# A fused retention and hard-swish MLP kernel: Q 1 to 3 are sent later, together, and GpSimd casts two of them

## The chip, the cores and the metric

The kernel runs on one core of one Trainium2 chip. The metric is device microseconds of one execution, as a median over runs. The core has five engines that run on their own and wait for each other through semaphores: TensorE (PE, matrix products; PEld is its weight load), VectorE (DVE), ScalarE (ACT), GpSimd (POOL) and SyncE (SP). SP only issues DMAs here. GpSimd issues the DMAs that convert from float32 to float16 on the way.

## The reference

For 8 batches, 8 heads, 576 positions and a head dimension of 64, a retention layer without softmax, and then an MLP over all 4608 tokens (512 features, 2048 hidden):

```python
scores = scale * np.matmul(q, k.transpose(0, 1, 3, 2))      # scale = 1/8
gamma = 1.0 - 2.0 ** (-5.0 - np.arange(H))
Dmat = np.where(rel >= 0, gamma[:, None, None] ** rel, 0.0)  # rel = row - column
x = np.matmul(scores * Dmat, v)                              # tokens x 512
h = x @ w_in
out = (h * np.clip(h + 3.0, 0.0, 6.0) / 6.0) @ w_out
```

## The kernel before, in words

Each batch's first 512 positions are cut into four pieces of 128; the 64 positions left over in each batch are worked on in pairs of batches at the end. Piece c has tiles `kn` (K), and `qv` (Q in its first half, V in its second), all in float16 with positions on the partitions. The decay is split into a factor on Q and one on V, so that within a piece only a causal mask is left. What earlier pieces of the batch give is carried in a 64 x 64 state per head (`tbd`, as a block diagonal of two heads).

A piece goes through these steps:

- `k_by_pe(c)` transposes K on TensorE (tile `trk`), and ScalarE copies the result to `qk`.
- `q_by_pe(c)` multiplies Q with `dq`, an identity whose diagonal is the decay factor, which transposes and scales in one step (`trq`); ScalarE copies that to `qk` too. `dq` is made by VectorE near the start (L175).
- `scores(c)` makes K times Q (`sc`), and VectorE multiplies it with the mask (`at`).
- `scale_v(c)` scales V on VectorE. `state_early(c)` adds K times V to the state (`u`, through `gfull` to `tbd`).
- `inter(c)` and `intra(c)` give the output of the piece (`o`) from the state and from the masked scores, and ScalarE copies it to `xt`, the input of the MLP.

The four pieces of batch 0 (`EARLY = 4`) go first, written out by hand at L795 to L823; the last of them has its own versions `scores_last` and `out_last`, which mask and copy in two halves. Then the MLP of the first 512 tokens begins: `g1_first` and `g1` are the product with `w_in` (L577, 64 matmuls for a block of 512 tokens, four for each 128 hidden features), ScalarE and VectorE make the activation (L585, L586), and `g2` is the product with `w_out` (L635). From the third block on, `g2_seven` forms that product from seven instead of eight block products (L720). The pieces of later batches are placed between the matmuls of the MLP by hand.

The whole order is fixed by the program text (`manual_schedule`): each engine carries out its own instructions in the order in which they are written, and an instruction that waits holds up all that follow it on its engine. That holds for the DMA issues, too. GpSimd issues, in this order, K and V of pieces 0 to 3 (`load_kv`), then `w_in` in five blocks (`load_win`, 256, 256 and three times 512 hidden features), two blocks of `w_out`, piece 4, the rest of `w_out`, and the later pieces. Each of its issues also waits for the landing of the eighth issue before it. Q of pieces 0 to 3 (`load_q`) comes over SP in float32 into `qf`, and ScalarE casts it to `qv` (`cast_q`, L128). Before the change Q 0 and Q 1 are issued at once, Q 2 behind the transposes of Q 0, Q 3 behind those of K 0.

`warm(n, 512)` has TensorE multiply zeros, so that it does not stand idle.

At the end, the last block of tokens (`last`) keeps the accumulator `x` in two banks, `xo` and `xtu`, and `copy_half(u)` copies and stores each. The rows of this block belong to two batches, so `store_quarter` and `store` write each tile with two DMAs, one issued by SP and one by ScalarE.

Of the kernel before, what the change touches and what calls it, by code (L numbers as in the profile page):

```python
# [13 lines left out]
ALU = mybir.AluOpType  # L14
# [3 lines left out]
def kernel(  # L18
# [106 lines left out]
                reason="the first pieces have the queues")  # L125

    def cast_q(c):
        nc.scalar.copy(loaded[c]["q16"], plain_q[c])  # L128

    def load_win(f0, f1):  # L130
        return nc.gpsimd.dma_start(
# [11 lines left out]
    nc.gpsimd.iota(wide, pattern=[[1, P + 1]], base=-1, channel_multiplier=-1,  # L143
                   allow_small_or_imprecise_dtypes=True)
    load_q(0)
    load_q(1)
    load_kv(0)
    zeros = const.tile([P, MBLK], FP16)
    nc.vector.memset(zeros, 0.0)
# [6 lines left out]
    for h in range(H):  # L156
# [15 lines left out]
    nc.vector.tensor_tensor(out=ident16, in0=mask01, in1=mask_wide[:, 0:P], op=ALU.subtract)  # L172

    dq = const.tile([P, H, P], FP16)
    nc.vector.tensor_tensor(out=dq, in0=ident16[:, None, :].to_broadcast([P, H, P]),  # L175
                            in1=gq[:, :, None].to_broadcast([P, H, P]), op=ALU.mult)
    gqv = const.tile([P, 2, H, D], FP16)
    cast_q(0)
    nc.scalar.copy(gqv[:, 1], gv[:, :, None].to_broadcast([P, H, D]))
# [10 lines left out]
    nc.vector.memset(gfull, 0.0)  # L190

    def fill_gfull():
        nc.scalar.copy(gfull[0:HALF, :, 0:D],
                       gc[0:HALF, 0, :, None].to_broadcast([HALF, NPAIR, D]))
        nc.scalar.copy(gfull[HALF:P, :, D:2 * D],
                       gc[HALF:P, 0, :, None].to_broadcast([HALF, NPAIR, D]))

    def fill_gq():
        nc.scalar.copy(gqv[:, 0], gq[:, :, None].to_broadcast([P, H, D]))
# [52 lines left out]
    def k_by_pe(c, tag=None):  # L252
        kn = loaded[c]["kn"]
        pk = bank_or(tag, [P, NPAIR, P], FP16, name=f"trk_{c}")
        for p in range(NPAIR):
            newest[0] = nc.tensor.transpose(pk[:, p, :], kn[:, 2 * p:2 * p + 2, :], ident16)
        nc.scalar.copy(qk_of(c)[:, 1], pk)

    def q_by_pe(c):
        q16, qk = loaded[c]["q16"], qk_of(c)  # L260
        pq = bank([P, NPAIR, P], FP32, name=f"trq_{c}")
        for p in range(NPAIR):
            for h2 in range(2):
                r = slice(h2 * HALF, h2 * HALF + HALF)
                newest[0] = nc.tensor.matmul(
                    pq[r, p, :], q16[:, 2 * p + h2, :], dq[:, 2 * p + h2, :],
                    start=(p == 0), stop=(p == NPAIR - 1), skip_group_check=True)
        if c == EARLY - 1:
            for p in (0, 2):
                nc.scalar.copy(qk[:, 0, p:p + 2], pq[:, p:p + 2])  # L270
        else:
            nc.scalar.copy(qk[:, 0], pq)

    def scores_last(c):

# [60 lines left out]
    def scores(c, late=9):  # L336
        run_later(late)
        qk = st[c]["qk"]
        sc = psum.tile([P, 2, NPAIR, P], FP32, tag="sc", name=f"sc_{c}")
        for p in range(NPAIR):  # L340
            for h2 in range(2):
                r = slice(h2 * HALF, h2 * HALF + HALF)
                nc.tensor.matmul(sc[:, h2, p, :], qk[r, 1, p, :], qk[r, 0, p, :],
                                 start=True, stop=True)
        at = work.tile([P, 2, NPAIR, P], FP16, tag="at", bufs=3, name=f"at_{c}")
        st[c]["at"] = at
        later.append(lambda: nc.vector.tensor_tensor(
            out=at.rearrange("t a b s -> t (a b) s"), in0=sc.rearrange("t a b s -> t (a b) s"),
            in1=mask_b, op=ALU.mult))
# [328 lines left out]
    def store_quarter(kb, i, j, src):  # L678

        cols = slice(NH * j, NH * j + NH)  # L680
        if kb < B:
            r0 = kb * S + TH * i
            nc.sync.dma_start(out[r0:r0 + TH, cols].rearrange("(u p) n -> p u n", u=2), src)
        else:
            rest = out.rearrange("(m x s) n -> x s m n", x=2, s=S)
            for x in range(2):
                queue = nc.scalar if x else nc.sync
                queue.dma_start(rest[x, MAIN:S, 2 * i:2 * i + 2, cols],
                                src[x * HALF:x * HALF + HALF])

    def g2_seven(kb, last=False):

        gt = gts[kb]

        def w(i, j):
            return wout16[:, KH * i:KH * i + KH, NH * j:NH * j + NH]

        def a(i, j):
            return gt[:, KH * j:KH * j + KH, TH * i:TH * i + TH]

        def s(name):
            return sums[kb, name]

        acc = {}

        def get(name):
            if name not in acc:
                if last and name == "x":
                    acc[name] = [psum.tile([P, NH], FP32, tag=t, name=f"x{t}_{kb}")
                                 for t in ("o", "tu")]  # L710
                else:
                    whole = bank([P, 2, NH], FP32, name=f"{name}_{kb}")
                    acc[name] = [whole[:, 0], whole[:, 1]]
                    wholes[name] = whole
            return acc[name]

        def product(name, u, left, right, first):
            dst = get(name)[u]
            for c in range(KH):
                newest[0] = nc.tensor.matmul(  # L720
                    dst, left()[:, c, P * u:P * u + P], right[:, c, :],
                    start=(first and c == 0 and (u == 0 or name not in wholes)),
                    stop=(c == KH - 1), skip_group_check=True)

        kept, wholes = {}, {}

        def parts(name, tile):
            if name in wholes:
                return [(wholes[name], tile)]
            return [(acc[name][u], tile[:, u]) for u in range(2)]  # L730

        def keep(name):
            kept[name] = work.tile([P, 2, NH], FP32, tag="keep_" + {"m5": "m1"}.get(name, name), bufs=1,
                                   name=f"keep_{name}_{kb}")
            for src, dst in parts({"m5": "z"}.get(name, "x"), kept[name]):
                nc.scalar.copy(dst, src)

        def total(i, j, name, src):
            osb = work.tile([P, 2, NH], FP32, tag="osb", bufs=4, name=f"osb_{kb}_{i}_{j}")
            for (a0, dst), (_, a1) in zip(parts(src, osb), parts(src, kept[name])):  # L740
                nc.vector.tensor_tensor(out=dst, in0=a0, in1=a1, op=ALU.add)
            store_quarter(kb, i, j, osb)

        def copy_total():
            osb = work.tile([P, 2, NH], FP32, tag="osb", bufs=4, name=f"osb_{kb}_1_0")
            nc.scalar.copy(osb, wholes["x"])
            store_quarter(kb, 1, 0, osb)

        def copy_half(u):
            osb = work.tile([P, NH], FP32, tag="osb", bufs=4, name=f"osh_{kb}_{u}")  # L750
            nc.scalar.copy(osb, acc["x"][u])
            store(kb, 2 + u, slice(0, NH), osb)

        def unit(name, u, left, right, first, then=()):
            def do():
                product(name, u, left, right, first)
                for f in then:
                    f()
            return do

        plan = [
            ("x", lambda: a(0, 0), w(0, 0), True, [lambda: keep("m1")]),
            ("y", lambda: a(0, 1), w(1, 0), True,
             [lambda: total(0, 0, "m1", "y"), lambda: token_sums(kb, "s3")]),
            ("x", lambda: s("s2"), wts["t2"], False, [lambda: keep("u2")]),
            ("z", lambda: s("s1"), wts["t1"], True,
             [lambda: keep("m5"), lambda: token_sums(kb, "s4")]),
            ("x", lambda: s("s3"), wts["t3"], False, [lambda: total(1, 1, "m5", "x")]),
            ("z", lambda: s("s4"), w(1, 1), False, [lambda: total(0, 1, "u2", "z")]),
            ("x", lambda: a(1, 1), wts["t4"], False, [] if last else [copy_total]),  # L770
        ]
        units = []
        for n, (name, left, right, first, then) in enumerate(plan):
            for u in range(2):
                after = then if u else []
                if last and n == len(plan) - 1:
                    after = [lambda u=u: copy_half(u)]
                units.append(unit(name, u, left, right, first, after))
        return units
# [3 lines left out]
    WQ = DFF // 4  # L783
    for c in range(1, EARLY):
        load_kv(c)
    load_win(0, WQ // 2)
    load_win(WQ // 2, WQ)
    for i in range(1, 4):
# [3 lines left out]
            load(4)  # L792
        load_wout(4 * i, 4 * i + 4)

    scale_v(0)  # L795
    q_by_pe(0)
    load_q(2, newest[0])
    warm(2, MBLK)
    cast_q(1)
    k_by_pe(0)  # L800
    load_q(3, newest[0])
    fill_gfull()
    for c in range(EARLY):
        if c:
            inter(c - 1)
# [1 line left out]
        if c < EARLY - 1:  # L807
            scores(c)
            run_later(9)
            if c:  # L810
                k_by_pe(c + 1)
            state_early(c)
            run_later(9)
            if not c:
                k_by_pe(c + 1)
            q_by_pe(c + 1)
            if c + 2 < EARLY:
                cast_q(c + 2)
            scale_v(c + 1)
        else:  # L820
            scores_last(c)
# [280 lines left out]
```

## Time and profile before

| | us |
|---|---|
| median of 3 runs | 294.99 |
| the 3 runs | 293.27, 294.99, 295.82 |
| the profiled execution | 294.43 |
| its span | 292.6 |

The span runs from the first to the last instruction that the profiler shows; 1.8 us of the execution lie around it. All times within the kernel count from the start of the span. In it TensorE is busy for 281.1 us (96%), VectorE for 227.6, ScalarE for 169.1, GpSimd for 104.3, and the granted clock of TensorE is 1.00. Up to 18.16 us only the four first pieces are worked on; the MLP's first matmul starts at 18.17, and the last matmul ends near 287.7.

Queue 0 (software_dynamic) carries what GpSimd issues, queue 1 (hardware_dynamic) what SP issues. Packets of K, V and Q in queue 0 write 128 bytes, those of Q in queue 1 write 256. A share of 100% of 16 engines is one packet in work on each engine all the time; with several in work it is above that.

### The profile page before, as it was taken

What the parts mean: (1) busy time and instruction counts of PE and PEld (TensorE: products, weight loads), DVE (VectorE), ACT (ScalarE), POOL (GpSimd) and SP (SyncE); (2) the same over time, 40 slices, a digit from 0 to 9 for tenths busy, and PEclk for the clock granted to TensorE, in tenths of its full rate; (3) what the DMA queues carried; (4) which work ended last, traced back from release to release, by engine and by line L of the source; (5) the groups of instructions that cost most, each with busy time, mean ns of one, the idle gap of its engine ahead of it and who ended that gap; (6) DMA issues with size and microseconds to landing.
All of it is one profiled execution on the core that took longest, in us unless ns stands there. A gap on an engine that the chain in (4) does not pass through costs nothing.

```text
span 292.6 us, 8351 instructions
## 1 busy us (share of the span) xinstructions
PE 281.1 (96%) x3492; PEld 174.7 (60%) x3492; DVE 227.6 (78%) x377; ACT 169.1 (58%) x301; POOL 104.3 (36%) x130
## 2 busy tenths in 40 slices
PE   7699999999989999999999999999999999999993
PEld 2454445544544587458745874587458745874682
DVE  4858656798758997899789988998899588728860
ACT  6668537784357744774486448644864286338711
POOL 8753578159523432443234324455550000000000
PEclk9999999999999999999999999999999999999999
DMA  9999999999999989997999799979992240120014
GB/s 137 177 205 203 191 157 215 165 126 137 132 215 166 160 85 120 168 141 81 121 163 143 77 127 170 136 82 123 160 139 47 74 110 0 38 81 30 0 39 109
DMA packets 156631, 36.21 MB, mean 124 GB/s; under 512 B 143792, under 2 KB 155568, under 8 KB 156592
## 3 DMA queue, kind: packets, MB, share of 16 engines
q0 software_dynamic: 113104, 17.83, 89.3%
q1 hardware_dynamic: 42896, 17.31, 30.5%
q8 instruction: 27, 0.44, 0.7%
q10 hardware_dynamic: 592, 0.52, 0.5%
q14 instruction: 12, 0.10, 0.1%
HBM read 36.70 MB, written 9.44 MB: 158 GB/s over the span
## 4 chain that ended last, share of the span: by engine, by line
PE 91%; DMA 4%; POOL 2%; DVE 1%; issue 1%; ACT 0%; ACTq 0%; POOLq 0%
PE ph L577 41%; PE x L720 14%; PE pout L635 9%; PE z L720 8%; PE y L720 5%; DMA kn<-in_k_dram 3%; PE o L483 3%; PE sc L450 2%; PE o L504 1%; PE u L535 1%; PE ph L600 1%; POOL kn L103 1%; DMA out_dram<-osb 1%; PE xtu L720 1%; PE xo L720 1%
## 5 line engine op out<-in xcount | busy, mean ns | idle before, releaser
L577 PE MATMUL ph<-xt,win 128*128 128x512 f16 x560 | 122.3, 379 | 0.0
L586 DVE SCALAR_TENSOR_TENSOR gt<-u,ph 128x512 f16<-128x512 f32 x144 | 95.7, 685 | 22.6 <-ACT u L585 21.4
L585 ACT ACTIVATE u<-ph,cb 128x512 f32<-128x512 f32 x144 | 98.4, 688 | 25.7 <-PE ph L577 25.1
L577 PEld LDWEIGHTS <-win 128*128 128x128 f16 x560 | 54.7, 98 | 64.4
L103 POOL DMA_DIRECT2D kn<-in_k_dram x40 | 34.0, 850 | 40.7 <-PE ph L577 15.4
L103 POOL DMA_DIRECT2D qv<-in_v_dram x40 | 33.8, 846 | 38.8 <-PE ph L577 16.2
L720 PEld LDWEIGHTS <-sum_s 128*128 128x128 f16 x448 | 42.7, 98 | 5.3
L103 POOL DMA_DIRECT2D qv<-in_q_dram x36 | 30.2, 839 | 28.7 <-PE z L720 10.4
L720 PEld LDWEIGHTS <-gt 128*128 128x128 f16 x336 | 32.1, 98 | 5.5
L635 PE MATMUL pout<-wout,gt 128*128 128x512 f16 x128 | 29.6, 379 | 0.1
L720 PE MATMUL x<-wsum_t,sum_s 128*128 128x256 f16 x192 | 22.9, 273 | 0.0
L556 ACT CAST tm<-th 128x256 f16<-128x256 f32 x24 | 9.7, 405 | 20.3 <-DVE th L551 20.1
L635 PEld LDWEIGHTS <-gt 128*128 128x128 f16 x128 | 11.9, 98 | 13.2 <-issue 0.4
L456 DVE TENSOR_TENSOR at<-sc,mask 128x1024 f16<-128x1024 f32 x14 | 17.0, 1217 | 1.9 <-PE sc L450 1.9
L676 DVE TENSOR_TENSOR sum_s<-gt 128x1024 f16<-128x1024 f16 (+1 forms) x21 | 18.1, 864 | 0.2
L332 DVE TENSOR_TENSOR qv<-qv,gqv 128x1024 f16<-128x1024 f16 x26 | 17.8, 684 | 0.0
L514 ACT CAST xt<-o 128x512 f16<-128x512 f32 x28 | 15.0, 585 | 4.6 <-PE o L504 4.6
L567 DVE TENSOR_TENSOR ta<-u,th 128x256 f32<-128x256 f32 x24 | 10.2, 424 | 6.3 <-ACT th L554 5.2
L720 PE MATMUL z<-wout,sum_s 128*128 128x256 f16 x112 | 14.5, 274 | 0.0
L720 PE MATMUL y<-wout,gt 128*128 128x256 f16 x112 | 14.3, 273 | 0.0
L720 PE MATMUL z<-wsum_t,sum_s 128*128 128x256 f16 x112 | 13.6, 273 | 0.0
L720 PE MATMUL x<-wout,gt 128*128 128x256 f16 x96 | 11.5, 272 | 0.0
(118 smaller groups left out, 255.3 us busy)
## 6 DMA issues: line engine op xcount, KB each, us to landing
out_dram<-osb SPq DMA_DIRECT2D x32, 256.0 KB, 3.2
kn<-in_k_dram POOLq DMA_DIRECT2D x32, 128.0 KB, 5.9
qv<-in_v_dram POOLq DMA_DIRECT2D x32, 128.0 KB, 6.0
qv<-in_q_dram POOLq DMA_DIRECT2D x28, 128.0 KB, 5.9
wout<-in_moe_w_out_dram POOLq DMA_DIRECT2D x4, 512.0 KB, 15.2
win<-in_moe_w_in_dram POOLq DMA_DIRECT2D x3, 512.0 KB, 12.3
qf<-in_q_dram SPq DMA_DIRECT2D x4, 256.0 KB, 4.6
win<-in_moe_w_in_dram POOLq DMA_DIRECT2D x2, 256.0 KB, 8.3
```

Source lines behind the costliest of these rows:

```text
L103: loaded[c]["dma"].append(nc.gpsimd.dma_start(dst[p0:p0 + n], src[b, :, s0:s0 + n, :].rearrange("h s d -> s h d")))
L332: scaled = nc.vector.tensor_tensor(out=qv, in0=qv, in1=gqv, op=ALU.mult)
L456: nc.vector.tensor_tensor(out=at.rearrange("t a j p s -> t (a j p) s"), in0=sc.rearrange("t a j p s -> t (a j p) s"), in1=mask64[:, None, ...
L514: nc.scalar.copy(xt_at(cs[0], 0, 2 * P).rearrange("e p (j x s) -> e p j x s", j=2, x=2) [:, :, :, half, :], o[half].rearrange("e j p s -> ...
L556: nc.scalar.copy(tm, ta)
L567: nc.vector.tensor_tensor(out=ta, in0=st[c]["u"][1], in1=st[c]["sum"], op=ALU.add)
L577: newest[0] = nc.tensor.matmul(ph, win16[:, dmc, P * fc:P * fc + P], xt_of(kb)[:, dmc, :], start=(dmc == 0), stop=(dmc == NCC - 1))
L585: nc.scalar.activation(u, ph, ACTF.Relu, bias=cb[:, 0:1], scale=1.0 / 6.0)
L586: nc.vector.scalar_tensor_tensor(out=gts[kb][:, fc, :], in0=u, scalar=1.0, in1=ph, op0=ALU.min, op1=ALU.mult)
L635: nc.tensor.matmul(pout, gt[:, fc, P * mc:P * mc + P], wout16[:, fc, :], start=(fc == 0), stop=(fc == NFC - 1))
L676: nc.vector.tensor_tensor(out=s(which)[:, c0:c1], in0=x(), in1=y(), op=op)
L720: newest[0] = nc.tensor.matmul(dst, left()[:, c, P * u:P * u + P], right[:, c, :], start=(first and c == 0 and (u == 0 or name not in whol ...
```

## The change

- Q 1 is issued behind the making of the diagonal `dq`, and Q 2 and Q 3 right behind Q 1, without a wait of their own.
- The casts of Q 2 and Q 3 go from ScalarE to GpSimd, where they stand between the issue of V 3 and the first of `w_in`.
- The cast of Q 1 goes behind the copy of K 0 on ScalarE; the two fills of `gfull` go from ScalarE to VectorE; one more warming matmul stands behind the transposes of K 0.
- In piece 0, V is scaled behind the mask of the scores, and the state is updated behind the transposes of piece 1. In piece 2, the state comes first, and Q 3 is transposed before K 3; the copy that is cut into halves is that of K 3 instead of Q 3.
- In the last block of tokens, the second half of quarter (0,1) is stored by GpSimd instead of ScalarE, and the last copy, of `xtu`, is made by VectorE instead of ScalarE.
- `newest`, to which later loads are tied, is no longer set by `q_by_pe`, and is set by `scores`. The loads that use it come behind matmuls of L577 or L720, so that it holds the same instruction there.

```diff
     def cast_q(c):
-        nc.scalar.copy(loaded[c]["q16"], plain_q[c])
+        (nc.scalar.copy if c < 2 else nc.gpsimd.tensor_copy)(loaded[c]["q16"], plain_q[c])
...
     load_q(0)
-    load_q(1)
     load_kv(0)
...
-    nc.vector.tensor_tensor(out=dq, in0=ident16[:, None, :].to_broadcast([P, H, P]),
-                            in1=gq[:, :, None].to_broadcast([P, H, P]), op=ALU.mult)
+    load_q(1, nc.vector.tensor_tensor(
+        out=dq, in0=ident16[:, None, :].to_broadcast([P, H, P]),
+        in1=gq[:, :, None].to_broadcast([P, H, P]), op=ALU.mult))
+    for c in range(2, EARLY):
+        load_q(c)
...
     def fill_gfull():
-        nc.scalar.copy(gfull[0:HALF, :, 0:D],
+        nc.vector.tensor_copy(gfull[0:HALF, :, 0:D],
...
     (k_by_pe)
-        nc.scalar.copy(qk_of(c)[:, 1], pk)
+        if c == EARLY - 1:
+            for p in (0, 2):
+                nc.scalar.copy(qk_of(c)[:, 1, p:p + 2], pk[:, p:p + 2])
+        else:
+            nc.scalar.copy(qk_of(c)[:, 1], pk)
...
     (q_by_pe)
-        if c == EARLY - 1:
-            for p in (0, 2):
-                nc.scalar.copy(qk[:, 0, p:p + 2], pq[:, p:p + 2])
-        else:
-            nc.scalar.copy(qk[:, 0], pq)
+        nc.scalar.copy(qk[:, 0], pq)
...
     (store_quarter)
-                queue = nc.scalar if x else nc.sync
+                queue = (nc.gpsimd if j > i else nc.scalar) if x else nc.sync
...
         def copy_half(u):
-            nc.scalar.copy(osb, acc["x"][u])
+            if u:
+                nc.vector.tensor_copy(osb, acc["x"][u])
+            else:
+                nc.scalar.copy(osb, acc["x"][u])
...
     for c in range(1, EARLY):
         load_kv(c)
+    for c in range(2, EARLY):
+        cast_q(c)
     load_win(0, WQ // 2)
...
-    scale_v(0)
+    fill_gfull()
     q_by_pe(0)
-    load_q(2, newest[0])
     warm(2, MBLK)
-    cast_q(1)
     k_by_pe(0)
-    load_q(3, newest[0])
-    fill_gfull()
+    warm(1, MBLK)
     for c in range(EARLY):
...
             run_later(9)
-            if c:
-                k_by_pe(c + 1)
-            state_early(c)
-            run_later(9)
             if not c:
-                k_by_pe(c + 1)
-            q_by_pe(c + 1)
-            if c + 2 < EARLY:
-                cast_q(c + 2)
+                cast_q(1)
+            else:
+                state_early(c)
+                run_later(9)
+            if not c:
+                scale_v(c)
+            if c == EARLY - 2:
+                q_by_pe(c + 1)
+            k_by_pe(c + 1)
+            if c < EARLY - 2:
+                q_by_pe(c + 1)
+            if not c:
+                state_early(c)
+                run_later(9)
             scale_v(c + 1)
```

More of the change, by code (lines that the diff above doesn't have):

```diff
@@ L192, in fill_gfull @@
     def fill_gfull():
-        nc.scalar.copy(gfull[0:HALF, :, 0:D],
-                       gc[0:HALF, 0, :, None].to_broadcast([HALF, NPAIR, D]))
-        nc.scalar.copy(gfull[HALF:P, :, D:2 * D],
-                       gc[HALF:P, 0, :, None].to_broadcast([HALF, NPAIR, D]))
+        nc.vector.tensor_copy(gfull[0:HALF, :, 0:D],
+                              gc[0:HALF, 0, :, None].to_broadcast([HALF, NPAIR, D]))
+        nc.vector.tensor_copy(gfull[HALF:P, :, D:2 * D],
+                              gc[HALF:P, 0, :, None].to_broadcast([HALF, NPAIR, D]))
     def fill_gq():
@@ L264, in q_by_pe @@
                 r = slice(h2 * HALF, h2 * HALF + HALF)
-                newest[0] = nc.tensor.matmul(
-                    pq[r, p, :], q16[:, 2 * p + h2, :], dq[:, 2 * p + h2, :],
-                    start=(p == 0), stop=(p == NPAIR - 1), skip_group_check=True)
-        if c == EARLY - 1:
-            for p in (0, 2):
-                nc.scalar.copy(qk[:, 0, p:p + 2], pq[:, p:p + 2])
-        else:
-            nc.scalar.copy(qk[:, 0], pq)
+                nc.tensor.matmul(pq[r, p, :], q16[:, 2 * p + h2, :], dq[:, 2 * p + h2, :],
+                                 start=(p == 0), stop=(p == NPAIR - 1), skip_group_check=True)
+        nc.scalar.copy(qk[:, 0], pq)
     def scores_last(c):
@@ L342, in scores @@
                 r = slice(h2 * HALF, h2 * HALF + HALF)
-                nc.tensor.matmul(sc[:, h2, p, :], qk[r, 1, p, :], qk[r, 0, p, :],
-                                 start=True, stop=True)
+                newest[0] = nc.tensor.matmul(sc[:, h2, p, :], qk[r, 1, p, :], qk[r, 0, p, :],
+                                             start=True, stop=True)
         at = work.tile([P, 2, NPAIR, P], FP16, tag="at", bufs=3, name=f"at_{c}")
```

## The prediction

> **What bounds the kernel now.** I read the page first, then the chain of waits for the first 20 us, then the DMA queues over short windows, then the timeline of the last ten microseconds.
>
> ```profile
> span 292.6 us, 8351 instructions
> ...
> PE 91%; DMA 4%; POOL 2%; DVE 1%; issue 1%; ACT 0%; ACTq 0%; POOLq 0%
> ```
>
> TensorE (PE) is the chain. From 18.2 us on it runs almost without a gap to 287.7; the diff leaves that part alone, so its 269 us are a block that can only be shifted. What the diff touches is the start, up to the first matmul of the MLP (L577), and the end, after the last one. The start's chain, in order of time (start, length, what):
>
> ```profile
> 6.75 7.55 DMA kn<-in_k_dram
> ...
> 14.34 0.40 PE trk L256 x4
> ...
> 15.18 0.34 PE trq L265 x8
> ...
> 16.20 0.37 PE sc L283 x8
> ...
> 16.59 1.30 DVE at L286 x2
> ...
> 18.23 1.83 PE ph L577 x8
> ```
>
> K 3 is the last load to matter: it is issued at 6.75 and lands at 14.30, and 3.8 us of transposes, scores and masks follow it. Why it takes 7.55 us is in the queues. First window 6 to 7 us, then 7.5 to 9 (queue, packets, MB, share):
>
> ```profile
> q0 software_dynamic: 1175, 0.15, 232.6%
> ...
> qf<-in_q_dram SPq DMA_DIRECT2D x1, 256.0 KB, 6.8
> ```
>
> ```profile
> q1 hardware_dynamic: 888, 0.23, 96.3%
> q0 software_dynamic: 428, 0.05, 55.9%
> ```
>
> Queue 0 (GpSimd's loads) alone moves 1175 packets per us. With a Q of queue 1 beside it the sum falls to 1316 in 1.5 us, 877 per us (948 in the window 10.5 to 12). A load of K, V or Q is 1024 packets, so the engines are full from 1.9 to 13.65 us with eight K and V and four Q. The same bytes move after the change; only their order can help.
>
> The end (timeline: start, length, engine):
>
> ```profile
> 284.71 2.64 ACTq L688 DMA_DIRECT2D out_dram<-osb  x2
> ...
> 285.80 1.04 PE L720 MATMUL xo<-wsum_t,gt 128*128 128x256 f16 x8
> ...
> 286.67 1.04 PE L720 MATMUL xtu<-wsum_t,gt 128*128 128x256 f16 x8
> 287.45 0.37 ACT L751 COPY osh<-xo 128x256 f32<-128x256 f32 x1 [4.30 <-DMA out_dram<-osb]
> ...
> 288.49 0.37 ACT L751 COPY osh<-xtu 128x256 f32<-128x256 f32 x1 [0.66 <-ACT osh L751]
> 288.89 0.51 ACTq L625 DMA_DIRECT2D out_dram<-osh  x1
> ```
>
> The sums are ready at 286.84 and 287.71, yet ScalarE copies them at 287.45 and 288.49. Each copy starts 0.10 to 0.12 after ScalarE's own issue of a store ends (284.71 + 2.64 = 287.35; 287.86 + 0.51 = 288.37). The DMA named as releaser is a neighbour in time.
>
> **The end, part by part.** The second half of the store of quarter (0,1) moves from ScalarE to GpSimd, and the last copy moves to VectorE. ScalarE is then free when `xo` is done: copy at 286.9 instead of 287.45. VectorE, idle after 286.69, takes `xtu` at 287.74 (its L741 began 0.03 after `xtu` at 284.22). For that copy the trace has ScalarE's 0.37 and L741's 0.42 with two inputs; I take 0.42: store issued at 288.21 instead of 288.89. That is 0.68, and I count **0.65 gained**. GpSimd's store must not become last. It is issued at 286.72; a GpSimd load of 64 KB issued near 201 us landed after 3.0, so it lands at 289.7, against 290.4 for the last one (issue 288.21 plus 2.2, the median landing of such stores). If it needed over 3.7 us, as in the full queues of the start, the gain would be gone.
>
> **The start: the loads.** Q 1 is now issued after `dq`, which ends at 3.60 (2.37 + 1.23), and Q 2 and 3 follow at once on SP, 0.37 to 0.56 each: issues at 3.65, 4.2 and 4.7. Nothing else stands behind them on SP until the store near 42 us.
> - Queue 1 is empty from 2.97 (1024 packets at 1080 per us from 1.9), so queue 0, which began at 4.0, begins then. K 0 lands near 5.2 instead of 6.12. It is worth nothing: TensorE has its two warming matmuls until 6.2 in front of the transposes. They were hidden before by K 0 and are now the limit; the extra warming matmul lies under ScalarE's 0.59 copy.
> - In the trace the first packets of Q 2 come 2.0 us after its issue (5.33, then 7.3), those of Q 3 3.6. I take 2.0: 5.65. By then queue 0 has moved 2.68 x 1150 = 3080 packets (K 0, V 0, K 1).
> - From 7.3 to 12.3 the old kernel moved some 4930 packets, 986 per us, 42% of them queue 1's. With three Q waiting I take half: 3120 / 493 = 6.3 us, so queue 1 ends at 12.0. Landing is 1.1 to 1.5 us behind the last packet. Q 1 lands at 8.5, Q 2 at 10.6, Q 3 at 13.1. Bounds: 10.9 + 1.1 = 12.0 at the 592 per us of the window above, and 14.3 if each Q takes the 2.85 us that lay between the starts of Q 2 and Q 3.
> - K 2 then lands at 11.1 (it was 11.04), V 2 at 13.3 (12.85), K 3 at 14.4 (14.30), V 3 at 15.15 (15.1).
>
> **The start: GpSimd's casts.** They are in no row. From below stands VectorE's 0.42 for 512 elements, from above GpSimd's iota (129 elements in 0.24) scaled to 0.95; I take 0.66, the iota's slope over its 0.10 memset. Cast 2 ends at 11.3, and TensorE wants it at 12.0. Cast 3 ends at 13.8, wanted at 14.5. Behind them on GpSimd wait all of w_in, then w_out and pieces 4 to 7:
>
> ```profile
> 8.48 3.79 POOL L131 DMA_DIRECT2D win<-in_moe_w_in_dram  x5
> ...
> 20.71 0.75 POOL L136 DMA_DIRECT2D wout<-in_moe_w_out_dram  x1 [1.48 <-DMA win<-in_moe_w_in_dram]
> ```
>
> w_in's first issue goes from 8.48 to 13.85, its first packet (0.84 after the issue, as near 63 us, where the queue was empty) from 13.65 to 14.7: 1.05 later, with the engines idle for 0.85. Its third block landed at 20.5 (issue 9.96 + 10.5) and is wanted 3.46 after the first MLP matmul (16 matmuls of 0.216): at 21.6, slack 1.1 to 1.2. The second has 1.8, the fourth 2.1; later, Q 5 lands 1.3 before its use at 41.39. So the move costs **nothing in my sum**, with no cover left: each later microsecond costs one.
>
> **The start: the order of the work.** Cast 1 now stands behind the copy of K 0 on ScalarE and ends at 9.1; Q 1's transposes, the state update and the output of piece 0 (0.41 each) come after it, scores 1 at 10.4 instead of 9.52. That is hidden, since the next thing waits for K 2 at 11.1. The two fills of `gfull` leave ScalarE (0.80) for VectorE, which is idle from 5.2 to 7.1. Piece 2: transposes, two copies of 0.59, scores at 13.0; but VectorE scales V 2 first (13.3 + 0.42) and masks until 15.0 (it was 14.6). Piece 3: Q is transposed before K (0.41 off the tail of K 3), K at 14.9; ScalarE copies Q 14.95 to 15.55, then half of K, 15.9; TensorE's output of piece 2 waits for that mask, until 16.0; VectorE has the state (0.69) and V 3 (0.42) until 16.2. Scores until 16.4, mask at 16.5 instead of 16.59: **0.1 gained**. What the new order saves behind K 3 is given back in front of it.
>
> **Sum.** 0.65 + 0.1 + 0 = 0.75 less. The profiled execution took 294.43 (span 292.6 and 1.8 around it), which gives 293.7. The median of the three runs is 0.56 higher, 294.99, so on that footing **294.2**. Those runs spread over 2.55 us; about 1% (2.95) is what can be told from no change.
>
> **Rivals.**
> 1. *w_in too late* (slower). The Q take turns with queue 0 as in the old trace, Q 3 lands at 14.3 and its cast, at 0.95, ends at 15.25. w_in starts at 16.15, 2.5 late; its third block lands at 23.0, and the MLP, 3.46 in, stops for it: 1.3 behind the old time at that place. Less 0.65: 0.65 slower, **295.6**. It decides from a cast end of 13.95 on. For it: Q 3 needed 6.8 us with less queued. Against it: the three are now queued together, as Q 0 and Q 1 were, which ran from 1.9 to 4.1 with 56 packets of queue 0 between.
> 2. *Even sharing.* Q 1's packets come 1.2 us after issue, as the first Q's did, and split the engines from 4.85: queue 0 has 2160 packets then, K 2 ends at 10.9 and lands at 12.2; scores 2 at 13.9, masks until 15.55, the last mask at 16.95, 0.35 late. Less 0.65: **294.7**. Against it: in the window 6 to 7 queue 1 had none, though Q 2 was issued at 5.33. The Trainium skill (DMA: Bandwidth & Descriptors, Queues, rings and completion order) says that an engine takes the queues in turn, a packet of at most 64 descriptors each; by that rule this rival would hold, and this window does not agree with it.
> 3. *Less mixing* (faster). If the Q run in one piece, the 12,300 packets need 7.2 + 3.9 us and end at 13.0, K 3 lands at 13.6, Q 3 near 11, and the chain behind is 0.9 earlier: with the end 1.6 less, **293.4**. Against it: both mixed windows.
> 4. *No end gain.* GpSimd's store lands last, or the chain at the start takes what the end gives: **295.0**.
>
> **Chances.** My sum 0.37, rival 1 0.25, rival 2 0.13, rival 3 0.11, rival 4 0.14. With the spread of the runs, half of 2.55, around the outer cases and rival 1 growing with a slower cast: 292.9 to 296.4. Over 1% faster (below 292.0) needs more than rival 3: 0.04. Over 1% slower (above 297.9) needs w_in some 5 us late: 0.09. Within 1%: 0.87.
>
> **What would show it.** Right: Q 3's cast ends between 13 and 14, w_in is issued at once after it, the last masks start near 16.5 and L577 near 18.1 without a gap; the last store is issued near 288.2 if nothing shifts. Wrong: a gap in L577 between 19 and 26 that w_in ends (rival 1), K 2 after 12 (2), K 3 before 14 (3), a last landing that is GpSimd's (4). GpSimd casts above 1.5 us each would break the sum.

## The result, and the profile after

The changed kernel takes 296.61 us (median of 8 runs, 296.0 to 298.14) beside 293.94 for the kernel before (median of 8, 293.05 to 295.82): 1.0091 times as long, with a 95% interval of 1.0067 to 1.0115. The forecast of 294.2 and its range up to 296.4 were too low, and where a gain was forecast there is a loss. The profiled execution took 296.60.

First the span, the granted clock in 40 slices, and the shares of the chain by engine, from the page of after:

```profile
span 294.8 us, 8356 instructions
...
PEclk9599999999999999999999999999999999999999
...
PE 82%; DMA 12%; POOL 1%; DVE 1%; issue 1%; SPq 0%; ACT 0%; DVEq 0%
```

The span is 2.2 longer. DMA has 12% of the chain, where it had 4%, and the second slice (7.4 to 14.7 us) has a clock of 0.5. The chain of waits at the start of after (start, length, what) runs elsewhere than before:

```profile
4.67 10.02 DMA qf<-in_q_dram
14.69 0.05 issue
14.74 0.61 POOL qv L128
15.35 3.62 POOL win L131 x5
18.98 13.10 DMA wout<-in_moe_w_out_dram
...
32.38 12.49 DMA qv<-in_q_dram
```

It no longer goes through K 3. It is Q 3, issued at 4.67 and landed at 14.69, then its cast on GpSimd, then the issues of `w_in` behind that cast. From there it runs on through GpSimd's queue: the first load of `w_out` lands at 32.08, only then is Q 5 issued (32.38, before 28.29), the load lands at 44.87, and TensorE's transposes of Q 5 start behind it, at 44.91. What waits for these loads shows in the timeline of after from 15 to 46 us (start, length, engine; in brackets the idle time before and what ended it):

```profile
15.30 3.73 POOL L131 DMA_DIRECT2D win<-in_moe_w_in_dram  x5
...
19.78 3.63 PE L578 MATMUL ph<-xt,win 128*128 128x512 f16 x16
...
24.48 0.55 PEld L578 LDWEIGHTS <-win 128*128 128x128 f16 x4 [1.57 <-DMA win<-in_moe_w_in_dram]
24.49 0.82 PE L578 MATMUL ph<-xt,win 128*128 128x512 f16 x3 [1.08 <-DVE gt L587]
...
44.91 0.41 PE L271 MATMUL trq<-dq,qv 128*64 128x128 f16 x8 [0.58 <-DMA qv<-in_q_dram]
```

The MLP starts at 19.78 instead of 18.17. Its weight loads then wait for the third block of `w_in`, which landed at 24.44 (the stop that the matmul row puts down to `gt` is the same one). Later Q 5, which stands behind `w_in` and `w_out` in GpSimd's queue, stops TensorE for another 0.58.

Where the time went, each row as a difference of the same instruction in the two traces:

| what | before | after | added |
|---|---|---|---|
| first matmul of the MLP | 18.17 | 19.78 | +1.61 |
| the 17th matmul of the MLP, the first that needs the third block of `w_in` | 21.63 | 24.49 | +1.25 |
| first product with `w_in` of the second block of tokens (Q 5 in between) | 52.08 | 55.61 | +0.67 |
| last matmul's end (a wait near 85 us was 0.94, is 0.25) | 287.71 | 290.33 | -0.91 |
| from there to the end of the span | 4.94 | 4.47 | -0.47 |

The sum is +2.15. The first three rows give each delay to the place where it shows; they are not three savings that could be had one by one. The chain reaches the transposes of Q 5, at 44.91 instead of 41.39, without any matmul of the MLP in it. So an earlier start of the MLP alone would only have made the later stops longer; in one run below it starts 1.15 later than here, and Q 5 is reached at the same time.

Why the MLP starts late stands in the windows of after (window, length, busy time and count of PE, PEld, DVE, ACT, POOL, then granted clock, DMA share, GB/s):

```profile
6.83:9.58 2.75, 0.01 (x2) 0.00 (x1) 1.56 (x2) 0.62 (x1) 1.71 (x2) 0.76 1.84 196
9.58:15.30 5.72, 5.71 (x61) 3.80 (x61) 3.22 (x5) 2.90 (x5) 1.17 (x2) 0.52 1.81 145
```

and in its timeline:

```profile
8.89 0.62 ACT L128 CAST qv<-qf 128x512 f16<-128x512 f32 x1 [2.51 <-DMA qf<-in_q_dram]
9.58 0.61 PE L258 MATMUL trk<-ident,kn 128*128 128x128 f16 x4 [2.75 <-DMA kn<-in_k_dram]
...
14.74 0.61 POOL L128 CAST qv<-qf 128x512 f16<-128x512 f32 x1 [2.79 <-DMA qf<-in_q_dram]
...
16.57 0.40 PE L258 MATMUL trk<-ident,kn 128*128 128x128 f16 x4
...
18.20 1.29 DVE L287 TENSOR_TENSOR at<-sc,mask_wide 128x512 f16<-128x512 f32 x2 [0.29 <-PE sc L284]
```

TensorE stands idle for 2.75 us waiting for K 1 (landed 9.54, before 7.91). Then it is busy without a gap for 5.7 us, at a clock of 0.52: the four transposes take 0.61 where they take 0.40 at 16.57. So a backlog forms. K 3 lands at 15.73 (before 14.30), and its transposes start 0.84 behind that instead of 0.04. The queues say why the loads are late: from 5 to 14 us (queue, packets, MB, share)

```profile
q0 software_dynamic: 6009, 0.76, 131.2%
q1 hardware_dynamic: 3110, 0.78, 51.7%
```

are 1013 packets per us, of which the three Q have a third. The share was not even: from 5.5 to 9 us queue 1 moved 1792 of 3458 packets, from 9 to 13 us 1190 of 4119, and its last ones came after 14. And the engines that were full all the time before have nothing to do when GpSimd at last issues `w_in`; from 15.5 to 16.5 us:

```profile
DMA packets 64, 0.01 MB, mean 8 GB/s; under 512 B 64, under 2 KB 64, under 8 KB 64
```

At the end, the timeline of after:

```profile
289.29 1.04 PE L721 MATMUL xtu<-wsum_t,gt 128*128 128x256 f16 x8
289.49 0.37 ACT L755 COPY osh<-xo 128x256 f32<-128x256 f32 x1 [3.73 <-PE xo L721]
289.62 0.62 POOL L689 DMA_DIRECT2D out_dram<-osb  x1 [69.10 <-DVE osb L742]
...
290.37 0.43 DVE L753 COPY osh<-xtu 128x256 f32<-128x256 f32 x1 [1.06 <-PE xtu L721]
```

ScalarE copies `xo` as soon as it is done, VectorE copies `xtu` 0.04 after the last matmul, and the last store is issued 0.49 after it (1.18 before).

### The profile page after: what moved, and what is told of

Same layout as the page of the kernel before. It is cut to its first block, busy times and chain, and to the rows that moved or that the text cites. A ratio compares the mean times of both kernels' runs of the same rounds, so it can differ in the third digit from the quotient of the medians.

```text
span 294.8 us, 8356 instructions
## 1 busy us (share of the span) xinstructions
PE 283.1 (96%) x3493; PEld 175.8 (60%) x3493; DVE 228.8 (78%) x380; ACT 167.0 (57%) x296; POOL 105.9 (36%) x133
## 4 chain that ended last, share of the span: by engine, by line
PE 82%; DMA 12%; POOL 1%; DVE 1%; issue 1%; SPq 0%; ACT 0%; DVEq 0%
PE ph L578 36%; PE x L721 14%; PE z L721 9%; PE pout L636 6%; PE y L721 5%; DMA wout<-in_moe_w_out_dram 4%; DMA qv<-in_q_dram 4%; DMA qf<-in_q_dram 3%; PE o L484 2%; PE sc L451 2%; PE o L505 1%; PE u L536 1%; PE ph L601 1%; POOL win L131 1%; PE xtu L721 1%; PE xo L721 1%
## 5 line engine op out<-in xcount | busy, mean ns | idle before, releaser
L689 POOL DMA_DIRECT2D out_dram<-osb x1 | 0.6, 617 | 69.1 <-DVE osb L742 69.1
L677 DVE TENSOR_TENSOR sum_s<-gt 128x1024 f16<-128x1024 f16 (+1 forms) x21 | 18.1, 863 | 0.2
L721 PE MATMUL z<-wout,sum_s 128*128 128x256 f16 x112 | 14.5, 274 | 0.0
L721 PE MATMUL y<-wout,gt 128*128 128x256 f16 x112 | 14.3, 274 | 0.0
```

The source lines that it names most:

```text
L677: nc.vector.tensor_tensor(out=s(which)[:, c0:c1], in0=x(), in1=y(), op=op)
L721: newest[0] = nc.tensor.matmul(dst, left()[:, c, P * u:P * u + P], right[:, c, :], start=(first and c == 0 and (u == 0 or name not in whol ...
```

## The experiments

Four theories, which may hold together. **H, the hold:** `w_in` stands behind a cast that waits for Q 3, so it is issued 6.8 us later. **S, the sends:** three Q queued together delay K 1, K 2 and Q 3, and the MLP starts late. **K, the clock:** most of what S costs comes from the halved clock, not from the landings. **C:** the cast is itself dear on GpSimd. The kernels of one group shared one chip and the runs of the kernel before (medians 294.63, 294.56 and 294.88); ratios are against that kernel.

### First group: each part by itself

**The end alone**, in the kernel before:

```diff
-                queue = nc.scalar if x else nc.sync
+                queue = (nc.gpsimd if j > i else nc.scalar) if x else nc.sync
...
-            nc.scalar.copy(osb, acc["x"][u])
+            if u:
+                nc.vector.tensor_copy(osb, acc["x"][u])
+            else:
+                nc.scalar.copy(osb, acc["x"][u])
```

> The kernel before with the two edits of its end alone: the second half of the store of quarter (0,1) by GpSimd, the copy of xtu by VectorE. If the end of the changed kernel gains what its trace shows (from the last matmul to the end of the span 4.47 us, before 4.94), this kernel is 0.45 to 0.65 us faster than before, a ratio of 0.998, with the last store issued 0.5 us behind the last matmul instead of 1.18. If the end costs (GpSimd's store lands last), it is at 1.000 or above. The first MLP matmul stays at 18.2 in both cases.

Measured: 0.9982 (0.9957 to 1.0008), 294.19 us. The last store is issued 0.50 after the last matmul, as in after. A gain of half a microsecond fits, but is not told from none.

**The changed kernel with the casts back on ScalarE:**

```diff
-        (nc.scalar.copy if c < 2 else nc.gpsimd.tensor_copy)(loaded[c]["q16"], plain_q[c])
+        nc.scalar.copy(loaded[c]["q16"], plain_q[c])
...
-    for c in range(2, EARLY):
-        cast_q(c)
...
+            if c + 2 < EARLY:
+                cast_q(c + 2)
```

> The changed kernel with the casts of Q 2 and Q 3 back on ScalarE, behind the transposes of Q 1 and of Q 2; the Q are still sent together. Theory H (w_in is held behind the casts): w_in is issued from 8.5 again, its third block lands before 22, TensorE does not stop in the first MLP product, and piece 5 is not late at 45; 1.8 us of the loss go, and the rest, some 0.9, stays, because the first MLP matmul is still near 19.5. Theory S (sending the three Q together is the whole loss, by making K, V and Q late): the first MLP matmul stays at 19.5 to 20 and so does nearly the whole loss, a ratio of 1.007 or more. Theory O (the new order of the work is slower by itself): the same as S here.

Measured: 1.0053 (1.0026 to 1.0079), 296.18 us. `w_in` is issued from 8.47 and no product waits for it, nor for Q 5, yet the MLP starts at 20.18. TensorE is idle from 7.11 to 9.88 and then has a clock of 0.5. That is S without H.

**The changed kernel with the sends as before:**

```diff
+    load_q(1)
...
-    load_q(1, nc.vector.tensor_tensor(
...
-    for c in range(2, EARLY):
-        load_q(c)
...
     q_by_pe(0)
+    load_q(2, newest[0])
...
     k_by_pe(0)
+    load_q(3, newest[0])
```

> The changed kernel with the Q sent as before (Q 1 at once, Q 2 behind the transposes of Q 0, Q 3 behind those of K 0), and the casts still on GpSimd ahead of w_in. Theory H: Q 3 lands near 13.4 as before, its cast ends near 14.1, w_in starts 1.2 us late instead of 3; the third block lands near 21.7 and TensorE stops for 0.2 to 0.5 us; together with the end, -0.5 to +0.2 us against before. Theory S: the whole loss goes, the first MLP matmul is at 18.2 or earlier, a ratio of 0.996 to 0.999. Theory O: the loss stays, the first MLP matmul above 19.

Measured: 1.0076 (1.0050 to 1.0103), 296.72 us. Here the MLP starts on time and then stops for `w_in`. GpSimd's and TensorE's timelines of this kernel:

```profile
13.46 0.61 POOL L128 CAST qv<-qf 128x512 f16<-128x512 f32 x1 [2.11 <-DMA qf<-in_q_dram]
14.02 3.73 POOL L131 DMA_DIRECT2D win<-in_moe_w_in_dram  x5
```

```profile
18.17 1.90 PE L577 MATMUL ph<-xt,win 128*128 128x512 f16 x8
20.97 1.90 PE L577 MATMUL ph<-xt,win 128*128 128x512 f16 x8 [0.90 <-DMA win<-in_moe_w_in_dram]
23.51 0.82 PE L577 MATMUL ph<-xt,win 128*128 128x512 f16 x3 [0.65 <-DMA win<-in_moe_w_in_dram]
```

That is H without S. It is also nearly what the prediction took for its own case (`w_in` from 13.85, at no cost); the second block, said to have 1.8 of slack, came 0.9 late. Q 5 then stops TensorE for another 0.84, until 44.31. The clock was halved in this profile, too, from 9.9 to 13.3, but the MLP starts at 18.17 as before, and the three other runs, with a mean granted clock of 1.00, took 295.91 to 297.66. So the clock is not what this kernel loses by.

**Both back**, so that the new order of the work and the end remain (the edits of the last two):

> The changed kernel with both the sending and the casts as before: what is left is the new order of the work and the end. Theories H and S: the loss is gone; the first MLP matmul lies between 17.6 and 18.2, no stop in the first product; 0.5 to 1.1 us faster than before, a ratio of 0.996 to 0.998. Theory O: slower than before by 0.5 or more, the first MLP matmul after 18.7. H beside S: H expects this one 0.2 to 0.5 us below the kernel with the sends alone put back; S expects no difference.

Measured: 0.9979 (0.9960 to 0.9998), 293.57 us, MLP from 17.84. So neither the new order nor the end costs anything. Against this kernel, S alone adds 0.74% and H alone 0.97%, and the changed kernel with both is 1.1% above it (its ratio is from another chip). They overlap, because one path ends last: where `w_in` is held, the landing of Q 5 sets the place at 44 us (44.31 with the sends as before, 44.91 in after), and a late start of the MLP lies under it.

### Second group: what makes the hold and the sends dear

**Both casts behind all five issues of `w_in`**, otherwise as changed:

```diff
-    for c in range(2, EARLY):
-        cast_q(c)
     load_win(0, WQ // 2)
...
         load_win(i * WQ, i * WQ + WQ)
+    for c in range(2, EARLY):
+        cast_q(c)
```

> The changed kernel with the five issues of w_in ahead of the two casts on GpSimd instead of behind them; the Q are sent together as in the changed kernel. Theory H (the hold of w_in is a cost of its own): no stop of TensorE in the first MLP product, which still begins at 19.5 to 20.2; the time is that of the kernel with the casts back on ScalarE, a ratio near 1.005, below the changed kernel's 1.009. Theory C (it is the cast on GpSimd itself that costs, by its length or by getting in the way of VectorE, wherever it stands): no better than the changed kernel, 1.008 or more.

Measured: 1.011 (1.0057 to 1.0162), 298.38 us. GpSimd's timeline shows that the test missed its aim:

```profile
11.84 0.74 POOL L131 DMA_DIRECT2D win<-in_moe_w_in_dram  x1 [1.07 <-DMA qv<-in_v_dram]
13.64 0.74 POOL L131 DMA_DIRECT2D win<-in_moe_w_in_dram  x1 [1.06 <-DMA kn<-in_k_dram]
14.38 1.38 POOL L128 CAST qv<-qf 128x512 f16<-128x512 f32 x2
```

The fourth and fifth issue of `w_in` wait for earlier landings, and now the casts wait behind them. Q 2, landed at 10.68, is cast at 14.38; TensorE loses 1.04 to that, and the MLP starts at 21.79. The hold is turned round.

**TensorE kept busy** in the kernel with the casts back:

```diff
             if not c:
+                warm(11, MBLK)
                 cast_q(1)
```

> The kernel with the Q sent together and the casts on ScalarE, with eleven more warming matmuls (of zeros) behind the scores of piece 0, which fill 2.4 us of the 2.77 us in which TensorE stood idle. Theory K (the halved clock from 8.8 to 15.7 that followed this idle time makes a good part of the 2.0 us by which the MLP begins late): the granted clock stays at 1.0, the transposes of Q 3 begin 0.3 to 0.8 us earlier, the first MLP matmul comes before 19.6, and the ratio falls from 1.0053 to 1.003 or 1.004. Theory L (the late landing of Q 3 and K 3 alone sets the start): the clock stays up and the first MLP matmul is still within 0.2 us of 20.2, the ratio near 1.005.

Measured: 1.0014 (0.9983 to 1.0045), 295.19 us. Two windows of the kernel with the casts back, then the same two of this one:

```profile
7.11:9.88 2.77, 0.00 (x1) 0.01 (x1) 1.56 (x2) 0.62 (x1) 2.77 (x4) 0.81 1.75 186
9.88:15.70 5.82, 5.81 (x61) 3.88 (x61) 3.27 (x5) 3.75 (x7) 2.79 (x5) 0.50 1.98 162
```

```profile
7.11:9.88 2.77, 2.44 (x15) 1.01 (x14) 1.23 (x2) 0.62 (x1) 2.77 (x4) 1.00 1.81 186
9.88:15.70 5.82, 4.78 (x80) 3.12 (x78) 4.10 (x6) 4.16 (x8) 3.39 (x6) 1.00 1.98 167
```

DMA share and GB/s hardly change, but with zeros to multiply the clock stays at 1.00, and the second window holds 80 matmuls instead of 61. The MLP starts at 18.92 instead of 20.18. Of the 2.34 us that the sends cost at that place (17.84 with both back), 1.26 went with the clock. Not all of that need be the clock's, since K 3 landed about 0.7 earlier in the second profile (15.1 beside 15.8); in the first its transposes start 1.14 behind its landing. The other runs agree: the mean granted clock was 0.994 to 1.000 in the ten runs of this kernel and 0.985 to 0.994 in the eight with the casts back. K holds there for about half of what the sends cost, not for most of it, and the intervals of the two ratios (1.0014 and 1.0053) still overlap.

**The sends as before, the casts between the issues of `w_in`** (on top of the kernel with the sends as before):

```diff
-    for c in range(2, EARLY):
-        cast_q(c)
     load_win(0, WQ // 2)
...
         load_win(i * WQ, i * WQ + WQ)
+        if i == 1:
+            cast_q(2)
+    cast_q(3)
```

> The kernel with the Q sent as before and the casts on GpSimd, but cast 2 behind the third block of w_in and cast 3 behind the fifth, so that no issue of w_in waits for a Q. Theory H: the whole loss of the kernel with the casts ahead of w_in (1.0076) goes, 0.9960 to 0.9985, the same as with the casts on ScalarE (0.9979) or up to 0.3 us better because ScalarE is relieved of two casts. Theory C (GpSimd's cast costs by itself): above 1.002.

Measured: **0.9948 (0.9926 to 0.9971)**, 293.71 us. This version beats both kernels. GpSimd still does both casts, so C falls: the price was the place in the queue. Its interval overlaps those of the kernels with the end alone and with both back, so no gain from the casts on GpSimd themselves is shown.

**Q 1 at once, Q 2 and 3 behind `dq`,** in the kernel with both back:

```diff
-    nc.vector.tensor_tensor(out=dq, in0=ident16[:, None, :].to_broadcast([P, H, P]),
+    load_q(2, nc.vector.tensor_tensor(out=dq, in0=ident16[:, None, :].to_broadcast([P, H, P]),
...
+    load_q(3)
...
-    load_q(2, newest[0])
...
-    load_q(3, newest[0])
```

> The kernel with the new order of the work, the new end and all casts on ScalarE (0.9979), with Q 1 sent at once as before, and Q 2 and Q 3 behind the diagonal without further waits. Two parts of the sending are told apart: if the lateness of Q 1 and K 1 (8.9 and 9.5 instead of 5.3 and 7.9, the idle time of TensorE and the halved clock) makes the loss, this kernel is within 0.3 us of 0.9979, with no idle time above 1.2 us. If the crowding by Q 2 and Q 3, which delays K and V behind them, makes it, K 2 lands after 12, K 3 after 15, and the first MLP matmul at 18.8 or later, a ratio of 1.001 or more.

Measured: 1.0015 (0.9985 to 1.0045), 295.26 us. TensorE's timeline of its profiled run:

```profile
11.06 0.61 PE L258 MATMUL trk<-ident,kn 128*128 128x128 f16 x4 [3.34 <-DMA kn<-in_k_dram]
```

K 1 comes at 11.01, later still than in after, although Q 1 is no longer late. Q 2 and Q 3 in queue 1 hold it up: from 6 to 9 us queue 1 moved 1673 packets and queue 0 1255. So it is the crowding by Q 2 and Q 3 that this profile shows, with Q 1 in time. Over all runs the loss against 0.9979 (both back) is smaller than the profiled run's 296.38 shows, and the two intervals just overlap.

### Third group: the two causes apart

**The changed kernel, kept busy** (the 11 warming matmuls, as above):

> The changed kernel, whole, with the eleven warming matmuls behind the scores of piece 0 that kept the clock up in the kernel with the casts on ScalarE (there 1.0053 fell to 1.0014). Theory H (in the changed kernel the held w_in sets the time, and the late start behind it is hidden): the clock stays at 1.0 and the MLP begins up to 1 us earlier, at 18.8 to 19.5, but the third block of w_in still lands at 24 to 24.5, the stop in front of it grows by as much, and the ratio stays at 1.0075 to 1.009. Theory K (the halved clock is what the changed kernel loses by): the ratio falls to 1.005 or less, as it did there.

Measured: 1.009 (1.0056 to 1.0123), 297.82 us, the ratio of the changed kernel. In the profiled run the clock fell anyway, later (14.5 to 18.0 us), and the MLP started at 20.93. The later start cost nothing: the product that needs the third block began at 24.39, beside 24.49 in after with a start 1.15 earlier, and its weight load had waited 0.29 for the block, so an earlier start would have gained next to nothing there. Q 5 stops TensorE for 0.68, until 44.90 (44.91 in after). The other runs take K out more cleanly than the profile does: in five of the seven the mean granted clock was 0.997 or more, and they took 296.26 to 298.52, while all eight runs of the changed kernel had 0.982 to 0.988. As long as `w_in` is held, the clock is not what the changed kernel loses by.

**The changed kernel with the casts between the issues of `w_in`:**

```diff
-    for c in range(2, EARLY):
-        cast_q(c)
     load_win(0, WQ // 2)
...
         load_win(i * WQ, i * WQ + WQ)
+        if i == 1:
+            cast_q(2)
+    cast_q(3)
```

> The changed kernel with cast 2 behind the third block of w_in and cast 3 behind the fifth; the Q are sent together, the casts are on GpSimd. This mends the test with both casts behind the fifth block, where cast 2 itself stood behind issues that wait for landings. Theory H: no stop in the first MLP product, the MLP begins near 20, and the ratio is that of the casts on ScalarE, 1.004 to 1.006. Theory C (GpSimd's cast costs wherever it stands): 1.008 or more.

Measured: 1.0037 (1.0011 to 1.0064), 296.37 us. TensorE's timeline:

```profile
19.91 11.40 PE L578 MATMUL ph<-xt,win 128*128 128x512 f16 x52
```

The start is as late as in after (19.78), but 52 matmuls follow without a stop up to the end of this window. Moving two casts by a few places in one queue takes 0.54% off the changed kernel's 1.0091, some 1.6 us. What is left is the sends': the kernel that differs from this one by the sends alone is at 0.9948.

**The best version, and the kernel with both back, kept busy:**

```diff
+                warm(3, MBLK)
                 state_early(c)
```

(at both places where `state_early` is called ahead of the last piece; one of them is passed twice, so the warming stands ahead of the state updates of pieces 0, 1 and 2.)

> The kernel with the Q sent as before and the casts on GpSimd between blocks of w_in (0.9948, its profile with a halved clock from 10.4 to 17.2 and the MLP at 20.1), with three warming matmuls each ahead of the state updates of pieces 0 and 1, where TensorE stood idle for 0.9 and 1.0 us. Theory K (idle time in this stretch decides whether the clock is halved): the clock stays at 1.0, the MLP begins at 17.5 to 18.1, and the time is 0.993 to 0.995 of before with less spread. If the halved clock of that profile was chance or doesn't matter, the ratio stays at 0.995; if the warming is in the way, above 0.997.

> The kernel with the new order and the new end, Q and casts as before (0.9979), with the same two groups of three warming matmuls. If taking two casts from ScalarE is worth something by itself, this one is 0.5 us or more above the one with GpSimd's casts between the blocks of w_in; if not, both are within 0.3 us of each other, at 0.994 to 0.998.

Measured: 1.0015 (0.998 to 1.005) and 1.0020 (0.9987 to 1.0053). By theory K the first was expected at 0.993 to 0.995; the second was expected at 0.994 to 0.998. Neither beats the version without them (measured on another chip: 0.9948 and 0.9979), and they do not differ from each other, so taking the two casts off ScalarE shows no gain. In the profiled run of the first the clock stayed at 1.00, as expected, but the MLP starts at 18.90 and not before 18.1: TensorE waits 0.62 for GpSimd's cast of Q 3. In the profiled run of the second, TensorE has a wait that this start does not explain:

```profile
106.57 1.78 PE L720 MATMUL x<-wsum_t,sum_s 128*128 128x256 f16 x11 [2.37 <-issue]
```

The clock was halved after it, from 107.4 to 110.8. Such waits near 104 to 108 us, of 0.28 to 2.37, appear in the profiles of the four kernels with added warming matmuls; why was not tested.

## Why the prediction was wrong, point by point

- **"So the move costs nothing in my sum" is the step that cost most.** It became 1.25 at the third block and 0.67 at Q 5, and by the chain above it sets the whole 3.5 us by which Q 5 is used late. The kernel with the sends as before tests it by itself: its cast ended at 14.07, near the forecast's 13.8, `w_in` was issued from 14.02, and it lost 0.97% against the kernel with both back. Two terms were too small. One is the first packet, put 0.84 behind the start of the issue. The row near 63 us that this comes from is

```profile
61.99 0.88 POOL L103 DMA_DIRECT2D kn<-in_k_dram  x1 [9.36 <-DVE qv L332]
```

  and its first packet comes at 63.7: the 0.84 runs from the end of that issue, which takes 0.88 itself. With `w_in` issued from 14.02 the first packets came 1.4 behind the start of the issue, at 15.4 (in after at 16.7, behind 15.30). The other is the third block of `w_in`, taken to land only as much later as the first packet, at 21.55; it landed near 23.5. Between 18 and 20 us the engines moved 109 and 95 GB/s there, where they moved 206 before; why is not shown. Q 5 landed at 44.3 (44.9 in after) instead of 40.1, and its cover was 1.3. The prediction's rival 1 named mechanism, place and sign ("a gap in L577 between 19 and 26 that w_in ends"), and its cast end of 15.25 is within 0.1 of the measured one. It had the third block at 23.0, and 24.44 was measured: it used the same two terms.
- **"I take half" failed, too.** The rate was right (986 per us forecast, 1013 measured; the old stretch that it was taken from has 5005 packets, 1001 per us, 41% of them queue 1's). The half held until 9 us; from there to 13 us queue 1 got 29%. At 12.0, where the forecast has it empty, it had moved 2816 of its 3120 packets, and the rest took until after 14. So Q 3 landed at 14.69, beyond the forecast's 13.1 and its own upper bound of 14.3 (5.65 and three times 2.85, with nothing for the 1.1 to 1.5 from the last packet to the landing), and its cast ended at 15.35 instead of 13.8. A row for a smaller share was in the prediction, 42% in the old trace, and it was set aside in favour of more for three queued Q.
- **K 1 was missing.** The prediction had K 0, V 0 and K 1 moved by 5.65 (3080 packets at 1150 per us), which would hide everything in piece 1. By 5.5 queue 0 had moved 1767; from 3.5 to 5.5 it ran at 800 per us with almost nothing of queue 1 beside it (1150 per us in the kernel before; why it was slower is not shown). The sum also has queue 1 empty at 2.97, where its own rate gives 2.85; 83 of its packets still came from 3 to 3.5. And the Q came from 5 on, nearer to rival 2's 4.85 than to 5.65. K 1 landed at 9.54 and TensorE waited 2.75. What follows was in no case of the prediction: the halved clock, and through it a backlog behind which K 3's transposes start. Rival 2 ("even sharing", K 2 at 12.2) came near on K 2, which landed at 12.85, but priced it at 0.35; the MLP's start was 1.61 late. By itself, without the hold, this part costs 0.74%.
- **GpSimd's cast** was sized well: 0.61 for 0.66.
- **The last masks** gained nothing (18.20 against 16.59) because all ahead of them was late. With both causes taken out, the new order brings the MLP to 17.84 instead of 18.17: the 0.1 was of the right sign.
- **The end** was right in mechanism: store issued 0.69 earlier behind the last matmul, forecast 0.68. The span gained 0.47 instead of 0.65, since the last store to land took 2.5 where 2.2 was taken. GpSimd's store landed 2.7 after its issue and was not the last.

## What to carry to other kernels

An operation that waits for a load does not belong ahead of DMA issues on the same engine: price it by the latest landing that it could wait for, and put it behind the issues whose data is needed first, but ahead of any issue that waits itself. Follow a late issue through the whole queue behind it: the load that cost most here was not the one held directly, but Q 5, used at 44.91. When loads are regrouped, ask which one becomes last on each queue, and take its share of the packets from the trace rather than from how many wait. A wait of TensorE early on may cost more than its length: look at the granted clock behind it.

## What the runs showed of the hardware that was not expected

- **The clock.** It fell to 0.5 for 6.8 us (8.2 to 15.1) beside an idle time of 2.75 in after, and likewise with 2.77 in the kernel with the casts back. The Trainium skill (TensorE: Matmul & The Clock Gate, HAM oscillation — how this bites in real kernels) puts the limit at gaps longer than about 3.4 us; here shorter ones were enough. The length of one idle time does not decide it alone, though, and what does is not shown. With both casts behind `w_in` the idle time was 2.76, too, and the clock stayed at 1.00 for almost 2 us behind it before it was halved (11.4 to 18.3). With the sends as before it fell (9.9 to 13.3) behind idle times of at most 0.73, and in the kernel before it stayed at 1.00 over 0.68 and 1.17. In the profiled run of the best version, 0.89 stood ahead of the fall and 0.97 in it:

```profile
6.00:10.40 4.40, 3.13 (x44) 1.86 (x45) 2.27 (x5) 2.21 (x6) 4.40 (x6) 1.00 1.96 162
10.40:17.20 6.80, 5.83 (x61) 3.67 (x58) 5.63 (x7) 2.47 (x5) 6.22 (x9) 0.50 1.73 194
```

  The MLP of that run starts at 20.13, and with 294.78 it was the slowest of its ten.
- **VectorE beside GpSimd's cast.** In the same run the scaling of V 1 on VectorE took 1.09 instead of the 0.41 of V 0 while GpSimd cast Q 2 from 10.77 to 11.44 (two rows of VectorE's timeline):

```profile
9.13 0.41 DVE L245 TENSOR_TENSOR qv<-qv,gqv 128x512 f16<-128x512 f16 x1
...
10.62 1.09 DVE L245 TENSOR_TENSOR qv<-qv,gqv 128x512 f16<-128x512 f16 x1
```

  By the Trainium skill (SBUF — State Buffer, SBUF: two separate sides) an operation of VectorE with two inputs in SBUF and one of GpSimd that reads SBUF shut each other out for a whole instruction. The length agrees: 0.68 more, beside a cast of 0.67. In after the scaling of V 2 took 0.71 beside the cast of Q 3. It is not always VectorE that waits: with the sends as before the same scaling of V 1, begun at 10.46, took 0.41, and the cast of Q 2, begun at 10.58, took 0.77 instead of 0.61.
- **A load of 256 KB** on queue 1 (Q 3 in after), behind two others and beside queue 0, took 10.02 us from issue to landing.
